# One written order for a whole half of the kernel, and late row blocks in rounded parts

## The chip, the cores and the metric

The kernel runs on one NeuronCore of a Trainium2 chip. The metric is the device time of one execution in microseconds (us); lower is better. The engines are TensorE (PE: matrix products; PEld: the loading of their weights), VectorE (DVE), ScalarE (ACT) and GpSimd (POOL). SyncE (SP) issues nearly all DMAs. Each engine works through its own queue in order, and engines wait for each other through semaphores. TensorE writes to PSUM, eight banks of 128 x 512 fp32; GpSimd doesn't touch PSUM here.

## The reference

```python
# x: 2048 x 512;  Wr, Wi: 2048 x 257;  w_gate, w_up: 512 x 1376;  w_down: 1376 x 512
h   = x + irfft2(rfft2(layernorm(x)) * (w_r + 1j * w_i))
n   = layernorm(h)
out = h + (gelu(n @ w_gate) * (n @ w_up)) @ w_down      # gelu: tanh form
```

All inputs and the output are fp32.

## The kernel before

The 2048 rows are 16 row blocks of 128 rows (row 16 p + b is partition p of block b). The work has four stages, each with an order that is written out as a list of short names; a name stands for one instruction or a few on one engine, and the list gives the order of each engine's queue.

1. START (to about 30 us): layer norm and the transform over the rows, with symmetric halves folded.
2. SECOND (to about 74 us): the transform over the columns, the product with the filter, and the way back over the rows' inner part. GpSimd and ScalarE meanwhile prepare the weights of hidden tiles 0 and 1.
3. FIRST (to about 121 us): the way back for row blocks 0 to 7 (the first half), the residual, the second layer norm, the transposition, and hidden tiles 0 and 1, each in two halves of 256 columns. `U8` to `U15` do the first step of the way back for the late blocks 8 to 15, and `K` unfolds three of them (8, 12, 9) on GpSimd: four 256-wide sums and differences, lines 830 to 833.
4. Two halves over rows. The first half (to about 279 us) multiplies row blocks 0 to 7 with hidden tiles 2 to 10 and adds up the down products; between these, the late blocks are finished. The second half does the same for row blocks 8 to 15, by an order of its own (SECOND_HALF), and ends at 438.6 us.

**A hidden tile.** The gate and up products of one tile of 128 hidden columns are seven block products (a Winograd form, for eight of the plain one), P0 to P6 (`products`, line 632). fp32 accuracy is reached by splitting each factor into a rounded high part (fp32r) and the remaining low part: `mm3` (lines 163 to 165) multiplies high x high, high x low and low x high. One block product is six matmuls of 128x128 by 128x512. A tile lies in three banks: 0 to 2 or 3 to 5, by turns. `tile_of` (line 664) has what follows each product: c1, c2, c3 copy a bank to SBUF (ScalarE, L673); d1, dy, d2 add (VectorE, L676); G0, G1 are gelu (ScalarE, L679); m0, m1 multiply (VectorE, L682); i0, i1 round the high parts (ScalarE, L688), and o0, o1 subtract for the low parts (VectorE, L695). P2 waits for c1, P4 for c2 and P5 for c3, since they add to the bank that was copied.

**A tile's weights** (`load_gu`, line 196). Two DMAs bring four raw blocks into one buffer (`raw`, a single one); GpSimd makes three more by four 256-wide sums (L207 to L215); in the first half VectorE then rounds all seven with one cast (L223), and GpSimd subtracts for the low parts in three steps, of 256, 768 and 768 columns (L228). With `by=act`, used in the second half, ScalarE rounds in three steps (L227), and each is followed by its subtract. `load_d` (line 504) loads a tile's down weights, rounds on ScalarE (L509) and subtracts on GpSimd (L511); three buffers.

**Down products** (`down`, line 754). Tiles are added up in groups (two tiles, then three, three, three). For each row block: three matmuls for each tile of the group into bank 6 or 7 (L769), then VectorE adds to `gh` (L775, or L772 with the output's DMA for the last group).

**Late blocks** (`late`, line 967). GpSimd unfolds (five of them here), SP loads the block's x, TensorE multiplies the block by the table `mis` in plain fp32 (L977: one product, which the trace shows as two records), VectorE adds the residual (L978) and takes the statistics (L520, L522). `normed` scales on ScalarE, and `combine` (line 545) transposes and makes the seven combinations `cb` for the second half.

**What sets the order there.** In the first half only TensorE's order is written (the loop at the end, lines 1243 to 1303, under `manual_schedule(engines={et.PE})`); the order on the other engines comes from a planner, with a few instructions tied to others by `issue_after` and `behind`. `rp` holds ten row buffers ("row"), given out in turn.

Of the kernel before, what the change touches and what calls it, by code (L numbers as in the profile page):

```python
# [20 lines left out]
P = 128  # L21
# [28 lines left out]
u0.1 u4.0 w4 C4.0 V4.2 X4 w0 C0.1 V0.3 X0 U1.2 C1.4 V1.0 X1 r0 U5.3 C5.5 V5.1 M4.1 O4.0 M0.2 O0.1 U2.3 H4 H0 X5 C2.5  # L50
V2.3 M5.1 H5 I4 G4 O5.0 G0 I0 S4 S0 A4 A0 E0.5 U7.2 C7.1 M1.3 O1.1 g0awh H1 Q0 N0 U6.0 C6.0 V7.4 X2 U3.4 C3.5 I5 G5 S5
M2.1 V6.3 R00 I1 G1 S1 A5 A1 R01 U9.7 C9 H2 X7 V3.1 X3 T00 a0 Q1 T01.2 s0.0 O2.1 U8.4 C8 E1.6 N1 R11 M7.0 c0 d0 f0
U12.3 e0.1 k0 R10 H7 b0 O7.0 g0 h0 C12 X6 M6.4 H6 i0 j0 T11.1 s1.2 r1 l0 T10 c1 d1 G2 I2 M3.2 O3.1 H3 G7 a1 b1 I7 S7
O6.0 U15.3 C15 e1.0 f1 g1 U14.5 C14 U10.4 C10 m0 k1 n1 g0aP0 g0ac1 g1aP0 l1 g0aP3 g0aP1 G3 I3 S3 A7 A3 Q3 g0aP2 I6 n0
G6 h1 g1ac1 E3.7 N3 g1aP2 i1 R31 T31.5 g1aP1 o1 R30 T30 S2 S6 A6 A2 g1ac2 j1 E2.6 Q2 N2 o0 g1aP4 g0awl s3.6 c3 g0ac2
g0aP4 R20 T20 a3 g1ac3 g1aP5 d3 e3.4 K9.5 m1 g0ad1 g0ac3 g0aP5 f3 b3 h3 g0ady g0aP6 i3 j3 R21 T21.7 g3 g1aP3 a2 b2
g0bP0 g0bP1 g1bP0 K12.4 g1ad1 g1ady g1aP6 r2 l3 k3 s2.8 g1aG0 c2 d2 f2 e2.7 k2 g1bP1 g1am0 g0bc1 g2 g0bP2 g1bc1 r3 n3
n2 o3 g1bP2 g0ad2 o2 g0aG0 g0am0 l2 m2 m3 g0bP3 h2 K8.4 g0aG1 g0am1 g0bc2 g0bP4 g1bd1 i2 j2 g1bc2 g1bP4 g1bG0 g1ad2
g0bc3 g0bd1 g0bdy g0ai0 g0ao0 g1aG1 g1bP3 g1ai0 g1am1 g1bc3 g1bdy g0ai1 g0ao1 g0bP6 g0bd2 g1awh g1awl g1ai1 g0bG1
g0bP5 hc g1bP6 lo1 lo2 g0bG0 g0bm0 g0bi0 g1bP5 g1bm0 g1bi0 g1bd2 g1bG1 g0bo0 U13.7 C13 lo3 g0bm1 g0bi1 U11.6 C11 g1bm1  # L60
g1bi1 g1ao0 g0bo1 g1bo0 g1bo1 g1ao1 g2P0
# [5 lines left out]
b7 b8 p15 f14 b9 h f15 b10 h b11 b12 b13 b14 b15 h  # L67
"""
# [51 lines left out]
def kernel(  # L120
# [75 lines left out]
    def load_gu(f, slowly=False, after=None, by=None, raw=None):  # L196
# [20 lines left out]
        if slowly:  # L217
            for m in range(7):
                split(r[:, 0, m], r[:, 1, m], t[:, m], pool)
                yield  # L220
        else:
            if not by:
                dve.tensor_copy(r[:, 0], t)  # L223
                yield
            for m in (slice(0, 1), slice(1, 4), slice(4, 7)):
                if by:
                    by.activation(r[:, 0, m], t[:, m], AF.Copy)  # L227
                pooled["lo"] = pool.tensor_tensor(r[:, 1, m], t[:, m], r[:, 0, m].bitcast(F32), op=ALU.subtract)  # L228
                yield
# [274 lines left out]
    def load_d(f, after=None):  # L504
        t = w3.tile([P, D], F32, name="wdr", bufs=1)
        nc.sync.dma_start(t, wd[f])
        wds[f] = r = w3.tile([P, 2, D], F32R, name="wd", bufs=3)
        with tc.issue_after(after.ins) if after else ExitStack():
            act.activation(r[:, 0], t, AF.Copy)  # L509
        yield  # L510
        pool.tensor_tensor(r[:, 1], t, r[:, 0].bitcast(F32), op=ALU.subtract)  # L511
        yield
# [203 lines left out]
    def gate_up(n):  # L716

        do = products(n)[1] if n == 2 else tile_of(n)

        def all_of(names):  # L720
            for k in names.split():
                ins = do[k]()
            return ins

        all_of("P0")
        if n == 2:

            yield
            do = tile_of(n)
            all_of("c1 P1 d1")  # L730
        else:
            all_of("c1")
            yield
            all_of("P1 d1")
        yield
        for names in ("P2 c2", "P3"):
            all_of(names)
            yield
        last = copied[n] = all_of("P4 c3")
        all_of("dy")  # L740
        yield

        for _ in load_d(tiles[n][1], last):
            pass

        for names in ("P5", "P6 d2"):
            all_of(names)
            k = names[1] == "6"
            with tc.issue_after(last.ins):
                do[f"G{k:d}"]()  # L750
            all_of(f"m{k:d} i{k:d} o{k:d}")
            yield

    def down(group, last):


        banks = {}

        def add(i, fs, c=slice(0, D)):

            b = i
            r = slice(i % 4 * P, (i % 4 + 1) * P)
            if fs[0] == group[0]:
                banks[i] = next(bank_67)
            o = ps[:, banks[i], : c.stop - c.start]
            for f in fs:
                for ha, hw in ((0, 0), (0, 1), (1, 0)):
                    start, stop = f == group[0] and ha + hw == 0, f == group[-1] and ha == 1
                    pe.matmul(o, parts_of[tiles.index((0, f))][:, ha, i // 4, r], wds[f][:, hw, c], start=start, stop=stop)  # L769
            if fs[-1] == group[-1]:  # L770
                if last:
                    dve.scalar_tensor_tensor(gh[:, b, c], o, mv[:, b, 0:1], gh[:, b, c], op0=ALU.add, op1=ALU.add)  # L772
                    nc.sync.dma_start(o3[:, b, c], gh[:, b, c])
                else:
                    dve.tensor_tensor(gh[:, b, c], o, gh[:, b, c], op=ALU.add)  # L775

        if last:

            for fs in (group[:-1], group[-1:]):
                for i in range(2):  # L780
                    add(i, fs)
                    yield
        for i in range(2 if last else 0, 7):
            add(i, group)
            yield

        add(7, group)
        yield

    tiles = [(q, f) for q, order in enumerate(orders) for f in order]  # L790
    downs = iter(())
    begun_tiles, wds, parts_of, hns, copied, sums = {}, {}, {}, {}, {}, {}
    bank_67 = itertools.cycle((6, 7))
# [150 lines left out]
    raw2 = load_gu(2)  # L944
    next(raw2)
    for k in ("r0", "r1", "r2", "r3", "hc", "lo1", "lo2", "lo3"):
        do[k] = lambda: next(raw2)

    def step(n):

        if n not in begun_tiles:
            f = tiles[n][1]
            if f not in gu:
                for _ in load_gu(f):
                    pass
            begun_tiles[n] = gate_up(n)
        next(begun_tiles[n])

    do["g2P0"] = lambda: step(2)
    et = mybir.EngineType  # L960
    with tc.manual_schedule(engines={et.PE, et.Activation, et.DVE, et.Pool}):
        for op in FIRST.split():
            name, *place = op.split(".")
            do[name](*map(int, place))


    def late(b):

        if b not in BY_THEN:

            with held("lo"):
                unfolded(b, row())
        yield
        xt = row()
        behind(nc.sync.dma_start(xt, x3[:, b]), pooled["raw"])
        py = ps[:, next(bank_67)]
        pe.matmul(py, mis[:, b], gh[:, b], start=True, stop=True)  # L977
        dve.scalar_tensor_tensor(gh[:, b], xt, mv[:, b, 0:1], py, op0=ALU.subtract, op1=ALU.add)  # L978
        for _ in stats2(b):
            pass  # L980
        yield

    def normed(b):

        hn = row()
        act.activation(hn, gh[:, b], AF.Copy, scale=rs2[:, b : b + 1])
        return hn

    def fill(n):
        for _ in range(n):  # L990
            next(downs, None)


    def second_half():
# [160 lines left out]
        yield  # L1155
# [86 lines left out]

    lates = {2: (9, 13), 3: (10,), 4: (14,), 5: (11,), 6: (15,)}
    ending = [late(b) for b in BY_THEN[:2]]
    for g in ending:
        next(g)
    downs = down(orders[0][:2], False)
    with tc.manual_schedule(engines={et.PE}):
        for n in range(2, NF):
            at_change = n == NF - 1  # L1250
            step(n)
            if n > 8:
                for i in range(2 * n - 18, 2 * n - 16):
                    with tc.issue_after(copied[n - 1].ins):
                        hns[i] = [normed(b) for b in (8 + i, 12 + i)]
            step(n)
            if at_change:
                second = second_half()
                with held("lo"):
                    next(second)  # L1260

                steps = [in_turn(i, hns[i], banks) for i, banks in enumerate(((3, 4), (5, 0), (3, 4), (1, 2)))]
                next(steps[0])
            for g in ending:
                next(g)
            if n in (6, 7):

                norm_scales(2 * n - 4, 2)
            if n == 7:
# [3 lines left out]
                for to, a in zip(kept_rows, (sd, mv[:, NB // 2 :, 0])):  # L1273
                    nc.sync.dma_start(to.rearrange("b n -> n b"), a)
# [155 lines left out]
```

## Time and profile before

| | us |
|---|---|
| median of three runs (lowest, highest) | 440.63 (440.52, 440.65) |
| the profiled execution's own time | 440.44 |
| its span, first to last instruction | 438.6 |

Busy times overlap between engines. A group's row has line, engine, operation, output<-inputs, shape and count, then busy time and mean duration in ns, then the idle time of the engine just before such instructions and what ended it. A row in order of time has start, duration, engine, line and operation; idle time before it and its releaser stand in brackets. Matmuls are pipelined: a 128x512 matmul's record is 0.39 us long, but the next one starts after 0.227, so the spacing is what TensorE pays. In the chain of waits each piece is given with the time that it adds.

### The profile page before, as it was taken

What the parts mean: (1) busy time and instruction counts of PE and PEld (TensorE: products, weight loads), DVE (VectorE), ACT (ScalarE), POOL (GpSimd) and SP (SyncE); (2) the same over time, 40 slices, a digit from 0 to 9 for tenths busy, and PEclk for the clock granted to TensorE, in tenths of its full rate; (3) what the DMA queues carried; (4) which work ended last, traced back from release to release, by engine and by line L of the source; (5) the groups of instructions that cost most, each with busy time, mean ns of one, the idle gap of its engine ahead of it and who ended that gap; (6) DMA issues with size and microseconds to landing.
All of it is one profiled execution on the core that took longest, in us unless ns stands there. A gap on an engine that the chain in (4) does not pass through costs nothing.

```text
span 438.6 us, 6625 instructions
## 1 busy us (share of the span) xinstructions
PE 432.1 (99%) x2275; PEld 366.6 (84%) x2275; DVE 313.3 (71%) x577; ACT 243.0 (55%) x502; POOL 314.5 (72%) x346
## 2 busy tenths in 40 slices
PE   8999999999999999999999999999999999999996
PEld 8998999789978777877888888888888888888885
DVE  5968976897864766368734579578677786687785
ACT  5989785799712442124432787376455653565640
POOL 6987896999859788648644944067879779787821
PEclk9999999999999999999999999999999999999999
DMA  8996904320022112112220203501212021200005
GB/s 290 386 414 105 360 27 143 129 73 24 25 96 97 49 55 89 48 50 72 72 73 24 72 25 120 169 11 62 73 48 72 26 71 49 72 24 2 0 2 192
DMA packets 23542, 41.60 MB, mean 95 GB/s; under 512 B 4178, under 2 KB 9810, under 8 KB 23380
## 3 DMA queue, kind: packets, MB, share of 16 engines
q1 hardware_dynamic: 23220, 40.92, 28.0%
q8 instruction: 18, 0.29, 0.3%
q10 hardware_dynamic: 288, 0.26, 0.2%
q14 instruction: 16, 0.13, 0.1%
HBM read 36.97 MB, written 4.20 MB: 94 GB/s over the span
## 4 chain that ended last, share of the span: by engine, by line
PE 90%; POOL 4%; DVE 1%; issue 1%; DMA 1%; ACT 0%; SPq 0%; DVEq 0%; POOLq 0%
PE ps L163 16%; PE ps L165 16%; PE ps L164 16%; PE ps L769 14%; PE ps L1108 11%; PE ps L425 4%; PE ps L437 3%; PE ps L464 3%; PE ps L530 3%; POOL pn L339 2%; POOL pn L338 2%; PE ps L869 2%; PE ps L977 1%; DMA gh<-in_x 1%; PE ps L1214 1%
## 5 line engine op out<-in xcount | busy, mean ns | idle before, releaser
L163 PE MATMUL ps<-cb,gu 128*128 128x512 f32 (+1 forms) x336 | 127.2, 379 | 0.3 <-DVE a L695 0.3
L165 PE MATMUL ps<-cb,gu 128*128 128x512 f32 (+1 forms) x336 | 124.9, 372 | 0.0
L164 PE MATMUL ps<-cb,gu 128*128 128x512 f32 (+1 forms) x336 | 124.8, 372 | 0.0
L673 ACT ACTIVATE s<-ps 128x512 f32<-128x512 f32 (+1 forms) x72 | 40.5, 562 | 87.1 <-PE ps L165 86.7
L228 POOL TENSOR_TENSOR gu<-raw,gu 128x768 fp32r<-128x768 f32 (+1 forms) x42 | 61.3, 1481 | 29.1 <-DVE gu L223 16.8
L163 PEld LDWEIGHTS ps<-cb,gu 128*128 128x128 f32 x336 | 63.3, 188 | 12.2 <-issue 1.0
L164 PEld LDWEIGHTS ps<-cb,gu 128*128 128x128 f32 x336 | 63.3, 188 | 11.8 <-issue 1.0
L165 PEld LDWEIGHTS ps<-cb,gu 128*128 128x128 f32 x336 | 63.3, 188 | 11.1
L769 PE MATMUL ps<-wd,a 128*128 128x512 f32 x264 | 63.6, 393 | 0.0
L769 PEld LDWEIGHTS ps<-wd,a 128*128 128x128 f32 x264 | 49.1, 188 | 11.6 <-DVE gh L978 1.0
L682 DVE TENSOR_TENSOR ps<-ps,s 128x512 f32<-128x512 f32 (+1 forms) x48 | 31.1, 651 | 28.1 <-PE ps L165 25.3
L1115 DVE TENSOR_TENSOR gh<-ps,gh 128x512 f32<-128x512 f32 x66 | 44.3, 682 | 0.8 <-PE ps L1108 0.8
L679 ACT ACTIVATE s<-s 128x512 f32<-128x512 f32 (+1 forms) x48 | 28.4, 594 | 20.8 <-DVE s L676 20.7
L775 DVE TENSOR_TENSOR gh<-ps,gh 128x512 f32<-128x512 f32 x24 | 16.6, 691 | 25.8 <-PE ps L769 25.8
L676 DVE TENSOR_TENSOR s<-ps,s 128x512 f32<-128x512 f32 (+1 forms) x48 | 30.7, 641 | 5.8 <-PE ps L165 4.7
L511 POOL TENSOR_TENSOR wd<-wdr,wd 128x512 fp32r<-128x512 f32 x12 | 15.6, 1298 | 17.1 <-ACT wd L509 17.1
L676 DVE TENSOR_TENSOR ps<-ps,s 128x512 f32<-128x512 f32 (+1 forms) x24 | 15.7, 654 | 16.1 <-ACT s L673 15.6
L688 ACT ACTIVATE a<-ps 128x512 fp32r<-128x512 f32 (+1 forms) x26 | 13.8, 533 | 17.1 <-DVE ps L682 17.1
L207 POOL TENSOR_TENSOR raw<-raw 128x256 f32<-128x256 f32 x16 | 11.9, 741 | 15.6 <-DMA raw<-in_wgu 13.9
L1021 POOL TENSOR_TENSOR t<-mis,t 128x768 fp32r<-128x768 f32 (+1 forms) x9 | 13.3, 1479 | 13.3 <-ACT t L1019 13.2
L429 ACT ACTIVATE dp<-ps 64x512 f32<-64x512 f32 x32 | 19.0, 593 | 4.0 <-PE ps L425 3.6
L453 POOL TENSOR_TENSOR z<-t,t 128x520 f32<-128x520 f32 x15 | 19.5, 1298 | 2.1 <-DVE t L445 2.1
(183 smaller groups left out, 896.7 us busy)
## 6 DMA issues: line engine op xcount, KB each, us to landing
wt<-in_w SPq DMA_DIRECT2D x16, 520.0 KB, 7.2
raw<-in_wgu SPq DMA_DIRECT2D x32, 256.0 KB, 3.0
out<-gh SPq DMA_DIRECT2D x15, 256.0 KB, 2.0
gh<-in_x SPq DMA_DIRECT2D x7, 512.0 KB, 8.8
row<-in_x SPq DMA_DIRECT2D x12, 256.0 KB, 2.8
wdr<-in_wd SPq DMA_DIRECT2D x12, 256.0 KB, 2.6
mis<-in_wd SPq DMA_DIRECT2D x10, 256.0 KB, 2.7
a<-in_wgu SPq DMA_DIRECT2D x8, 256.0 KB, 3.1
```

Source lines behind the costliest of these rows:

```text
L163: pe.matmul(o, lh, rh, start=(i == 0 and not onto), stop=False, skip_group_check=True)
L164: pe.matmul(o, lh, rl, start=False, stop=False, skip_group_check=True)
L165: last = pe.matmul(o, ll, rh, start=False, stop=(i == n - 1), skip_group_check=True)
L228: pooled["lo"] = pool.tensor_tensor(r[:, 1, m], t[:, m], r[:, 0, m].bitcast(F32), op=ALU.subtract)
L453: eng.tensor_tensor(z[:, :, first], t1[:, :, first], t2[:, :, first], op=ALU.add)
L673: return lambda: act.activation(to, a, AF.Copy)
L676: return lambda: dve.tensor_tensor(to, a, b, op=ALU.add)
L679: return lambda: act.activation(g, g, AF.Gelu_apprx_tanh)
L682: return lambda: dve.tensor_tensor(u, u, g, op=ALU.mult)
L769: pe.matmul(o, parts_of[tiles.index((0, f))][:, ha, i // 4, r], wds[f][:, hw, c], start=start, stop=stop)
L1108: pe.matmul(ps[:, k], w[:, hw], a[ha], start=start and hw + ha == 0, stop=hw == 1, skip_group_check=True)
L1115: by.tensor_tensor(to, o, to, op=ALU.add)
```

## The change

- FIRST is written in another order, without the cast of tile 2's weights (`hc`), which ScalarE now rounds too; its last entry, `g2P1`, stands for tile 2's c1, P1 and d1.
- A new list, FIRST_HALF, gives the order of TensorE, ScalarE, VectorE and GpSimd for the rest of the first half, in place of the written TensorE loop and the planner. FIRST and FIRST_HALF are issued under one `manual_schedule`.
- Names of the new list: `tNPk`, `tNc1` and so on are tile N's steps as above; `yN.0` to `yN.10` load and prepare tile N's weights (DMA; four sums on GpSimd; then ScalarE and GpSimd by turns, three times); `wN.0` to `wN.2` the down weights; `Kb` unfolds block b; `ub` rounds it (ScalarE) and `vb` makes its low part (GpSimd); `mh` and `ml` do the same once for the table (128 x 1024); `Lb` loads x, `Yb@k` is the block's product into bank k, now of three matmuls; `Rb` and `Bb` are residual and statistics; `Dgi@k` and `Egi` are the down product and the sum for row block i and group g (`F` the last tile's part); `H` and `i` are the scaling and the combinations, `N` the norm's scales, `S0` the rows kept for the second half, `Z` the second half's first loads.
- The rounded parts of a late block take two row buffers each. Rounded table parts lie in a tile `t`.
- The second half's own order is as before.

The diff, cut to its core (of the long lists, the stretches that matter below):

```diff
 FIRST = """
...
+g1bP2 g1aG0 e2.7 k2 n2 g1ad2 o3 g0bc2 h2 o2 m2 l3 i2 g0am0 g0bG0 g1bd1 g0bP3 g1bc2 g0bP4 g0ai1 g1aG1 j2
+g0bc3 g0bdy g1bP4 g1bP3 g0ai0 g1bc3 g1awh g0bP5 m3 g1am0 g0bP6 K8.4 lo1 g1ai0 g1bdy g1bG0 g1bP6 g0ao0 g1ao0 g0ao1
+g0bd2 lo2 lo3 U13.7 g0bG1 g1bP5 U11.6 g0bm0 g0bi0 g1bd2 g1bG1 g0bm1 g0bi1 g0bo0 g2P0 C13 g1am1 g1ai1 g1bm0 g1bi0 g0bo1
+g1awl C11 g1bm1 g1bi1 g1bo1 g1ao1 g1bo0 g2P1
 """
...
+FIRST_HALF = """
+u8 t2P3 t2P2 v8 mh ml Y8@6 u12 v12 y3.0 y3.1 y3.2 t2c2 L8 L12 u9 Y12@7 t2P4 R12 D01@7 y3.3 y3.4 R8 D00@6 y3.5 y3.6
+t2c3 t2dy t3P0 y3.7 y3.8 w2.0 t3P1 t2P5 y3.9 y3.10 E00 w2.1 w2.2 D02@6 t3c1 t3P2 v9 K13 y4.0 y4.1 B8.0 t3c2 B12.0 y4.2
+y4.3 E02 t2G0 t3P3 E01 D03@7 E03 t2P6 t3P4 t3d1 u13 v13 L9 L13 t2d2 t2m0 D04@6 B8.1 E04 y4.4 y4.5 y4.6 y4.7 y4.8 y4.9
+t2i0 y4.10 t3c3 D05@7 t3dy D06@6 E05 t4P3 K10 w3.0 D07@7 w3.1 w3.2 y5.0 t2o0 t4P0 t2G1 t2m1 t2i1 E06 t4c1 t3P5 t4P2
+u10 v10 E07 Y13@7 t3G0 t3m0 Y9@6 t2o1 t4P1 R13 y5.1 t4c2 B12.1 t4P4 t4d1 t4G0 R9 t3i0 t3P6 t3d2 L10 w4.0 K14 t4c3 t4P5
+y5.2 y5.3 u14 v14 y5.4 y5.5 Y10@6 Y14@7 w4.1 t4dy t4P6 y5.6 y5.7 t3o0 t5P0 t4m0 t4i0 t4o0 y5.8 t5P3 L14 R14 y5.9 y5.10
...
+L11 K15 t6P0 y7.0 y7.1 w5.0 y7.2 y7.3 y7.4 E13 t5P6 B14.1 t6c1 t4i1 t4o1 D15@7 t5d2 t5G1 t5m1 u15 t6P2 t6P1 E15 D14@6
...
+H11 H20 H21 t8G0 t8m0 w8.0 t9P0 t9c1 t7o1 D25@7 y10.0 D24@6 E24 y10.1 t8P6 y10.2 y10.3 y10.4 y10.5 y10.6 y10.7 t9P2
...
+"""
...
             for m in (slice(0, 1), slice(1, 4), slice(4, 7)):
                 if by:
                     by.activation(r[:, 0, m], t[:, m], AF.Copy)
+                    if apart:
+                        yield
                 pooled["lo"] = pool.tensor_tensor(r[:, 1, m], t[:, m], r[:, 0, m].bitcast(F32), op=ALU.subtract)
                 yield
...
-    raw2 = load_gu(2)
+    raw2 = load_gu(2, by=act)
...
-    def late(b):
-
-        if b not in BY_THEN:
-
-            with held("lo"):
-                unfolded(b, row())
-        yield
-        xt = row()
-        behind(nc.sync.dma_start(xt, x3[:, b]), pooled["raw"])
-        py = ps[:, next(bank_67)]
-        pe.matmul(py, mis[:, b], gh[:, b], start=True, stop=True)
-        dve.scalar_tensor_tensor(gh[:, b], xt, mv[:, b, 0:1], py, op0=ALU.subtract, op1=ALU.add)
...
-    with tc.manual_schedule(engines={et.PE}):
-        for n in range(2, NF):
...
+        def back_s(k):
+            nonlocal py
+            py = ps[:, k]
+            for hm, hu in ((0, 0), (1, 0), (0, 1)):
+                pe.matmul(py, mi2[:, hm, b - NB // 2], parts[hu], start=hm + hu == 0, stop=hu == 1)
...
+        def part(h):
+            parts[h] = rp.tile([P, D], F32R, name="row")
+            if h:
+                pool.tensor_tensor(parts[1], gh[:, b], parts[0].bitcast(F32), op=ALU.subtract)
+            else:
+                act.activation(parts[0], gh[:, b], AF.Copy)
...
+        mi2 = w3.tile([P, 2, NB // 2, P], F32R, name="t", bufs=1)
+        act.activation(mi2[:, 0], mis[:, NB // 2 :], AF.Copy)
+
+    later["mh"] = high_of_mi
+    later["ml"] = lambda: pool.tensor_tensor(mi2[:, 1], mis[:, NB // 2 :], mi2[:, 0].bitcast(F32), op=ALU.subtract)
...
+    with tc.manual_schedule(engines={et.PE, et.Activation, et.DVE, et.Pool}):
+        for op in FIRST.split():
+            name, *place = op.split(".")
+            do[name](*map(int, place))
+        for op in FIRST_HALF.split():
+            name, _, place = op.partition("@")
+            later[name](*([int(place)] if place else []))
     with tc.manual_schedule(engines={et.PE, et.Activation, et.DVE, et.Pool}):
         next(second, None)
```

## Prediction before the run

> **What bounds the kernel now.** I read the page's busy times first, then the busy time by stretch, then the groups by shape, the chain of waits, and last the instructions in order of time where TensorE waits.
>
> ```profile
> span 438.6 us, 6625 instructions
> ...
> PE 432.1 (99%) x2275; PEld 366.6 (84%) x2275; DVE 313.3 (71%) x577; ACT 243.0 (55%) x502; POOL 314.5 (72%) x346
> ```
>
> By stretch (the stretch, then PE, PEld, DVE, ACT and POOL busy with their instructions, then TensorE's clock and the DMAs):
>
> ```profile
> 116.00:168.00 52.00, 51.68 (x231) 40.81 (x230) 35.17 (x59) 16.85 (x33) 40.28 (x42) 1.00 0.25 81
> 168.00:220.00 52.00, 52.00 (x225) 41.96 (x224) 32.41 (x69) 14.74 (x26) 34.75 (x37) 1.00 0.18 56
> ```
>
> The reader is to see that TensorE is never idle in the stretches that the change rewrites, at full clock. So two things alone can move the time: work that TensorE no longer does, and waits that TensorE gets. In 116 to 168 us GpSimd has 12 us free of 52, ScalarE 35.
>
> **The work that goes.** Each late block's fp32 product becomes three products of rounded parts.
>
> ```profile
> 123.84 0.87 PE ps L977 x2
> ...
> 134.17 2.72 PE ps L769 x12
> ```
> ```profile
> L977 PE MATMUL ps<-gh,mis 128*128 128x512 f32 x16 | 7.8, 591 | 0.0
> ```
>
> The chain of waits gives 0.87 us for one fp32 product (two records) and 2.72 / 12 = 0.227 us for one product of rounded parts. Eight blocks: 8 x (0.87 - 3 x 0.227) = **1.5 us less**. Below I write 1.36 for a tile product (six of 0.227), 2.04 for a down product of nine, 0.68 for a late block.
>
> The Trainium skill (FP8 and Floating Point Precision, section TensorE Precision Notes) says that true fp32 makes four passes through the array, among them low times low. By that the change saves one pass of 0.227 a block, 1.8 us in all, and the sum would be 0.3 us lower; the row of 0.87 differs a little from four passes (0.91), and I go by the row.
>
> **The wait that goes.** At 119 us TensorE stands before tile 2's first product.
>
> ```profile
> 118.33 0.83 PE L530 MATMUL ps<-dis,gh 128*128 128x128 f32 x6
> 119.44 0.50 PE L163 MATMUL ps<-cb,gu 128*128 128x512 f32 x1 [0.27 <-DVE a L695]
> ```
> ```profile
> 115.92 2.14 DVE L223 CAST gu<-raw 128x1792 fp32r<-128x1792 f32 x1
> ...
> 118.97 0.41 DVE L695 TENSOR_TENSOR a<-ps,a 128x256 fp32r<-128x256 f32 x1
> ```
> ```profile
> 115.80 1.31 POOL L511 TENSOR_TENSOR wd<-wdr,wd 128x512 fp32r<-128x512 f32 x1
> ```
> ```profile
> L223 DVE CAST gu<-raw 128x1792 fp32r<-128x1792 f32 x9 | 10.9, 1207 | 2.4 <-PE ps L164 1.3 <-POOL raw L215 1.1
> ```
>
> The cast took 2.14 us beside a GpSimd subtract, against (10.9 - 2.14) / 8 = 1.10 for the other eight; VectorE came late to the low part that ended at 119.38, and TensorE started 0.06 later. The product's first matmul shows 0.50 where its followers show 0.39, so idle and slow start are 0.27 + 0.1 or a little more: **0.4 us less**, since ScalarE now rounds. What is late next there is the copy behind the product, which is in the next part.
>
> **Work that is only moved to idle engines.**
>
> ```profile
> L227 ACT ACTIVATE gu<-raw 128x768 fp32r<-128x768 f32 x10 | 8.4, 844 | 0.0
> ...
> L227 ACT ACTIVATE gu<-raw 128x256 fp32r<-128x256 f32 x5 | 2.0, 403 | 0.0
> ```
> ```profile
> raw<-in_wgu SPq DMA_DIRECT2D x32, 256.0 KB, 3.0
> ```
>
> Rounding a tile's weights costs ScalarE 0.40 + 2 x 0.84 = 2.1 us, some 19 for nine tiles, where VectorE paid 10.9; the eight 512-wide rounded parts 8 x 0.63 (the row of a 512-wide rounding below); the high part of the table (128x1024) between 0.84, its 768-wide row, and twice that. ScalarE's 35 free us cover these, except where one stands in front of something urgent (below). The loads are the same ones; the next raw tile lands in 3.0 us and its first user stands 5.4 us of GpSimd work behind it.
>
> **The work that comes.** GpSimd gets eight low parts of blocks (1.25 each) and the low part of the table. Of these, six and the table fall where 116 to 168 us is now: 40.3 + 6 x 1.25 + 2.4 = 50.2 of 52 us. So GpSimd has no reserve left just where it makes the tiles' low parts. I walked the new list there, and priced each step by these rows:
>
> ```profile
> 133.78 0.39 PE L165 MATMUL ps<-cb,gu 128*128 128x512 f32 x1
> ```
> ```profile
> 119.41 0.58 ACT L823 ACTIVATE gh<-ps 128x512 f32<-128x512 f32 x1
> 119.89 0.38 ACT L688 ACTIVATE a<-ps 128x256 fp32r<-128x256 f32 x1
> ...
> 134.21 0.60 ACT L673 ACTIVATE s<-ps 128x512 f32<-128x512 f32 x1 [9.73 <-PE ps L165]
> ...
> 188.44 0.63 ACT L509 ACTIVATE wd<-wdr 128x512 fp32r<-128x512 f32 x1 [2.39 <-PE ps L769]
> ```
> ```profile
> 127.57 0.68 DVE L775 TENSOR_TENSOR gh<-ps,gh 128x512 f32<-128x512 f32 x1
> 128.16 0.17 DVE L522 BATCH_NORM_AGGREGATE mv<-bn 128x2 f32<-128x6 f32 x1
> ...
> 134.84 0.70 DVE L676 TENSOR_TENSOR ps<-ps,s 128x512 f32<-128x512 f32 x1 [1.32 <-ACT s L673]
> ```
> ```profile
> 126.16 0.74 POOL L207 TENSOR_TENSOR raw<-raw 128x256 f32<-128x256 f32 x1 [3.69 <-DMA raw<-in_wgu]
> 126.98 0.74 POOL L211 TENSOR_TENSOR raw<-raw 128x256 f32<-128x256 f32 x1
> ...
> 189.15 1.30 POOL L511 TENSOR_TENSOR wd<-wdr,wd 128x512 fp32r<-128x512 f32 x1 [6.05 <-ACT wd L509]
> ...
> 301.37 1.30 POOL L1044 TENSOR_TENSOR a<-row,a 128x512 fp32r<-128x512 f32 x1 [1.40 <-ACT a L1039]
> 302.62 0.74 POOL L228 TENSOR_TENSOR gu<-a,gu 128x256 fp32r<-128x256 f32 x1
> ```
> ```profile
> L228 POOL TENSOR_TENSOR gu<-raw,gu 128x768 fp32r<-128x768 f32 x28 | 51.4, 1852 | 8.4 <-ACT gu L227 6.4 <-issue 1.9
> ```
>
> A last matmul at 133.78 lets its reader start at 134.21, 0.20 after its step of 0.227. ScalarE hands to VectorE 0.03 after its record's end, to GpSimd 0.08. Behind each other, ScalarE's 512-wide steps are 0.48 apart, VectorE's 0.60, GpSimd's 1.25; GpSimd's dependent 256-wide ones 0.82, its 768-wide ones 1.81 (0.04 less than their record, as with the 512-wide). The 1024-wide subtract has no row: 1.30 and 1.85 (512 and 768) extended give 2.4, two 512-wide ones 2.5.
>
> *Wait 1, block 8's products.* Zero is the end of t2P0. ScalarE copies (c1) at 0.20; u8 stands behind it: 0.68 to 1.31; v8 starts on GpSimd at 1.39, ml at 2.64 and ends at 5.04; TensorE could go on at 5.10. It reaches ml's product after t2P1, t2P3, t2P2 and one product: 4.31. It waits 0.8, and for v12 (ends 6.29, with TensorE there at 6.01) another 0.3: **1.1 us**.
>
> *Wait 2, tile 3.* GpSimd goes on at 6.24 with y3.1 to y3.4 (to 9.44), hands to ScalarE's y3.5 and gets it back: y3.6 is 9.95 to 10.69. ScalarE's y3.7 stands behind t2c3 and ends at 11.10; y3.8 runs 11.18 to 13.03. TensorE (P4, D01, D00 and t3P0 after Y12) is at t3P0 at 10.66 and at t3P1 at 12.1: waits of 0.1 and 1.0, **1.1 us**.
>
> *Wait 3, t4P2.* w3.1 rounds into a buffer that D07 frees, and holds ScalarE's queue: from D07's end w3.1 at 0.20, t2G1 at 0.72 to 1.35, VectorE's t2m1 to 2.07, t2i1 at 2.10, t4c1 at 2.58 to 3.18. TensorE has t4P0 and t3P5, 2.72: **0.5 us**.
>
> *Wait 4, t5P3.* From y3.8's end to y5.8's end GpSimd's queue holds four 768-wide steps (7.2), three blocks' unfolding (four 256-wide steps each, 8.7), six 512-wide steps (7.5) and ten 256-wide ones (7.5): 31 us, and some 3.3 us in which it waits for ScalarE or a row buffer (1.3 of it for u10, behind wait 3), so 34.2. TensorE needs 22 x 1.36 + 4 x 0.68 + 0.5 = 33.2: **0.8 us** (the difference less handover).
>
> *Wait 5, D15.* t6c1 waits for t6P0 and holds t4i1: 0.20 + 0.48 + 0.60 + 0.03, then t4o1 0.68 and handover 0.06 = 2.05, against one product, 1.36: **0.7 us**. *Wait 6, D25.* E22, t8m0 and t7o1 queue on VectorE: 0.20 + 0.60 + 0.60 + 0.68 + 0.06 = 2.14 against t9P0's 1.36: **0.8 us**.
>
> For none of these is there other TensorE work in the list to fill in, and lost TensorE time isn't regained later, as it stays at 99%. The second half keeps its order, and its first products find their inputs 0.4 us or more early by the same walk.
>
> The sum is -1.5 - 0.4 + 1.1 + 1.1 + 0.5 + 0.8 + 0.7 + 0.8 = +3.1. The profiled execution took 440.44 us around its span of 438.6, so it would become 443.5; the median of the runs shown is 440.63, 0.2 more, and would become **443.7 us**, my forecast.
>
> **The rivals.** *The waits don't arise* (faster): what decides is how early each feeder starts. If the engines run ahead of TensorE, no wait remains and the gain stands: 440.6 - 1.9 = 438.7. For it speaks that ScalarE is free two thirds of the time; against it that waits 1, 3, 5 and 6 each begin at a TensorE product and can't start earlier. It is faster by 0.2% (0.9 us) only if waits under 1.0 us remain in all.
> *GpSimd is quicker than its rows* (same): waits 2, 4 and the 0.3 of v12 go, the others stay: 443.7 - 2.2 = 441.5, and down to 440.7 with 0.8 off the rest. It takes a GpSimd some 10% shorter over 50 us, and the free 12 us of before speak for some room.
> *Row buffers* (slower still): the first half asks for 41 row buffers instead of 25, of ten; each TensorE wait frees them later, GpSimd and the loads stand behind, and tiles 6 to 8 get waits such as tile 5's, 2 x 0.8 to 1.0, so 1.8 in all: 445.5. For it speaks that the walk already shows GpSimd waiting for a row before K14; against it that its queue is some 5 us ahead at tile 6.
>
> The Trainium skill (SBUF — State Buffer, section Who interferes with whom) says that VectorE and GpSimd share one exclusively locked port pair, and that VectorE instructions with at most one SBUF input, outside two-port modes, stay clear of it. The slow cast above agrees; by that rule GpSimd's twelve added us (8 x 1.25 + 2.4) cost VectorE nothing once the casts are gone, so I add no price for it.
>
> **How the numbers follow.** The walk as it stands 0.70, row buffers 0.10, quicker GpSimd 0.10, no waits 0.10. The range reaches from the quicker GpSimd, 440.6, to the row buffers, 445.6; the walk's own is 442.0 to 445.0, with wait sums between 3.5 and 6.5. About 0.2% can be told from no change. Slower 0.80, same 0.10, faster 0.10.
>
> **What would show it.** Late blocks: 24 products of 0.227 instead of 16 fp32 records. No cast on VectorE, and none of the wait at 119. TensorE idle before the products of mi2 and rows, released by GpSimd, about 1.1; before L163 by GpSimd about 1.9; before the down products by VectorE 1.5; GpSimd over 95% busy for 50 us after tile 2 begins. TensorE without idle time in the first half makes the prediction wrong, and so does a second half that is longer than before.

## The result: 1.05 us slower, and a second half that got longer

| | before | after |
|---|---|---|
| median, nine runs each (us) | 440.63 | 441.68 |
| lowest, highest | 440.47, 440.98 | 441.58, 442.15 |
| ratio after to before | | 1.0024, interval 1.0014 to 1.0034 |

The forecast was 443.7: the sign is right, the size is a third of what was forecast, and as the following shows, the sum was wrong in more places than that says. In each later group of runs the kernel before took 440.55 to 440.65 us again. The head of the page of the changed kernel, and its busy time by stretch (columns as for the kernel before):

```profile
span 439.9 us, 6676 instructions
...
PE 432.8 (98%) x2283; PEld 368.1 (84%) x2283; DVE 303.5 (69%) x568; ACT 263.3 (60%) x538; POOL 327.1 (74%) x355
```
```profile
116.00:168.00 52.00, 51.26 (x238) 41.90 (x237) 26.47 (x50) 26.67 (x50) 48.89 (x47) 1.00 0.23 77
168.00:220.00 52.00, 52.00 (x229) 42.66 (x228) 29.18 (x61) 23.46 (x41) 38.68 (x41) 1.00 0.21 71
```

The work moved as forecast: VectorE 35.2 to 26.5 us in the first stretch, ScalarE 16.9 to 26.7, GpSimd 40.3 to 48.9 of 52 (50.2 was forecast). TensorE is idle for 0.74 us in all between 116 and 220 us. So most of the forecast waits (5.0 us in all) can't be there, and yet the time went up.

**Where the time went.** TensorE's last piece, and the first late product of the second half, in order of time, before and then after:

```profile
295.56 0.61 PE L1108 MATMUL ps<-row,t 128*128 128x512 f32 x2
...
433.72 0.76 PE L1214 MATMUL ps<-a,wd 128*128 128x256 f32 x5
```
```profile
295.66 0.62 PE L1029 MATMUL ps<-row,t 128*128 128x512 f32 x2
...
434.82 0.75 PE L1135 MATMUL ps<-a,wd 128*128 128x256 f32 x5
```

At the second half's first late product the changed kernel is 0.1 us behind; at the end, 1.1. The second half loses 1.0 us, though its order and its waits are those of before. The chain of waits shows it at the same products of the second half, before and after:

```profile
329.73 0.68 PE ps L1108 x3
331.76 0.68 PE ps L1108 x3
```
```profile
329.85 0.70 PE ps L1029 x3
331.93 0.70 PE ps L1029 x3
```

Three products take 0.70 us instead of 0.68, at a granted clock of 1.00 from 280 to 434 us in both kernels. At full resolution of the records the steps of 512-wide products are 226 or 227 ns nearly everywhere before; after, long stretches have steps of 224 to 237 ns, 230.5 to 231 in the mean. What these steps take over 226.7 ns adds up to 0.6 us from 116 us on before and 2.6 us after, 1.0 of it in the second half. After three or more steps of 226 or 227 ns, a longer one comes at 32 places, and in 29 of them the product reads `wd`.

What the change does to `wd`: a tile that the prediction passed over. The kernel before allocates `sd`, 32 bytes of each partition, after everything else; the changed kernel allocates it early, with 64 bytes, and the tiles behind it move up. The start addresses in a partition, as the program's allocation lists them:

```
tile   before            after
sd     227648 (behind)   213056
wd     215360            215424     (first of three, 4096 bytes apart)
gu      48192             48192     = 64 above a multiple of 256
cb     104512            104512     = 64 above a multiple of 256
row, t, a                            64 above a multiple of 256 in both
```

Before, every operand of the rounded products lies 64 bytes above a multiple of 256. After, `wd` alone lies 128 above. (`wdr`, the raw down weights, moves with it, but TensorE doesn't read it.)

### The profile page after: what moved, and what is told of

Read it like the earlier page. It is cut to its first block, busy times and chain, and to the rows that moved or that the text cites. A ratio compares the mean times of both kernels' runs of the same rounds, so it can differ in the third digit from the quotient of the medians.

```text
span 439.9 us, 6676 instructions
## 1 busy us (share of the span) xinstructions
PE 432.8 (98%) x2283; PEld 368.1 (84%) x2283; DVE 303.5 (69%) x568; ACT 263.3 (60%) x538; POOL 327.1 (74%) x355
## 4 chain that ended last, share of the span: by engine, by line
PE 91%; ACT 4%; DMA 2%; issue 1%; POOL 1%; SPq 0%; DVE 0%; DVEq 0%; ACTq 0%
PE ps L190 16%; PE ps L188 16%; PE ps L189 16%; PE ps L1227 14%; PE ps L1029 11%; PE ps L452 4%; PE ps L558 3%; PE ps L464 3%; PE ps L491 3%; DMA gh<-in_x 2%; PE ps L821 2%; PE ps L1135 1%; ACT ts L407 1%; PE ps L1198 1%; ACT ms L357 1%
## 5 line engine op out<-in xcount | busy, mean ns | idle before, releaser
L701 ACT ACTIVATE s<-ps 128x512 f32<-128x512 f32 (+1 forms) x72 | 40.3, 561 | 58.3 <-PE ps L190 58.0
L252 ACT ACTIVATE gu<-raw 128x768 fp32r<-128x768 f32 (+1 forms) x42 | 28.3, 697 | 10.9 <-DMA raw<-in_wgu 5.7
```

The source lines that it names most:

```text
L701: return lambda: act.activation(to, a, AF.Copy)
```

## The experiments

**e1, sd of 128 bytes.**

```diff
-    sd = w3.tile([P, NB], F32, name="sd", bufs=1)[:, : NB // 2]
+    sd = w3.tile([P, 2 * NB], F32, name="sd", bufs=1)[:, : NB // 2]
```

> The changed kernel with one number altered: the small tile sd takes 128 bytes of each partition instead of 64, so that the three wd tiles behind it begin 64 bytes above a multiple of 128, as in the kernel before and as every other operand of TensorE's rounded products; in the changed kernel they begin on a multiple of 128. Theory A (addresses): in the trace of the changed kernel the 512-wide steps of 228 to 236 ns begin, in 29 of 32 places, at a product that reads wd, and add up to 2.2 us over 227 ns a step, against 0.2 before. They go, and the time falls by 2.0 us to 439.7, below the kernel before (440.63). Rival B (traffic: GpSimd's and ScalarE's added work slows TensorE's reads): the work is the same, so the time stays at 441.7. Rival C (TensorE's clock is a little lower in this program): 441.7 too. By either theory the wait before the products of mi2 (1.1 us) stays.

Measured: 442.31 us, slower still (1.0037, 1.0025 to 1.0050). The period of 128 bytes was wrong; but the time did move with nothing altered than 64 bytes of an allocation, and the sum of the long steps rose from 2.6 to 3.4 us. Rivals B and C had no change to offer.

**e2, the kernel before with sd where the change has it.**

```diff
     do["g2P0"] = lambda: step(2)
+    sd = w3.tile([P, NB], F32, name="sd", bufs=1)[:, : NB // 2]
...
-                sd = w3.tile([P, NB // 2], F32, name="sd", bufs=1)
```

> The kernel before with one piece of the change alone: sd is allocated where the change allocates it and with its 64 bytes, ahead of wd, so that wd begins on a multiple of 128. Order and work are those of before. Theory A (addresses): 264 + 99 rounded products read wd, and steps of 228 to 236 ns appear at them: 440.63 + 2.0 = 442.6, in the second half about 1.1 of it. Rivals B and C: nothing that they speak of changes, 440.6.

Measured: 442.61 us (1.0045, 1.0032 to 1.0057), 2.0 more than before, as forecast. The same stretch of the chain, here of e2, has the long triples without any of the change's work:

```profile
326.70 0.68 PE ps L1109 x3
328.74 0.70 PE ps L1109 x3
330.81 0.70 PE ps L1109 x3
```

**e3, the down products of block 0 moved ahead of block 8's.**

```diff
-u8 t2P3 t2P2 v8 mh ml Y8@6 u12 v12 ... u9 Y12@7 t2P4 R12 D01@7 y3.3 y3.4 R8 D00@6 y3.5 y3.6
+u8 t2P3 t2P2 D00@6 v8 mh ml u12 v12 ... u9 Y8@7 t2P4 E00 Y12@6 R8 D01@7 y3.3 y3.4 R12 y3.5 y3.6
```

> The changed kernel with five names of its list moved: TensorE does the first block's down products (D00) before block 8's three products, and tile 2's fifth product between the products of blocks 8 and 12, so that GpSimd's low parts (ml, v8, v12) have 2.7 us more. Work and addresses are unchanged. Theory (the wait of 1.1 us before the products of mi2 is TensorE time lost, and nothing is behind it): 441.7 - 1.1 = 440.6. Rival (GpSimd is the bound over these 50 us, and the wait comes back at tile 3's first products, 131 to 134 us): 441.7, with the same 1.1 us before L188.

Measured: 441.31 us, 0.4 less than the changed kernel: between the two. The runs of both overlap a little (441.18 to 441.89, and 441.58 to 442.15), so the reading rests on the rows. The wait before block 8 is gone, and this has come before tile 3's products, in order of time:

```profile
130.71 0.39 PE L189 MATMUL ps<-cb,gu 128*128 128x512 f32 x1
131.12 0.50 PE L190 MATMUL ps<-cb,gu 128*128 128x512 f32 x1
...
132.38 0.39 PE L189 MATMUL ps<-cb,gu 128*128 128x512 f32 x1
132.92 0.50 PE L190 MATMUL ps<-cb,gu 128*128 128x512 f32 x1 [0.16 <-POOL gu L255]
```

Steps of 0.41 and 0.54 instead of 0.23, and a slow one behind each: 0.7 us. So GpSimd's work is the bound there. The forecast's waits 1 and 2 are one lack of GpSimd time; where wait 1 stands, it gives GpSimd what wait 2 would have asked for.

**e4, e1 and e3 together.**

> Both edits, the 128 bytes for sd and the moved down products. If addresses and the wait are two separate terms: 441.7 - 2.0 - 1.1 = 438.6, two us below the kernel before. If the address effect only fills time in which TensorE would wait for GpSimd anyway, less than the sum: 439.6 or more.

Measured: 441.95 us, 0.4 below e1, as e3 is 0.4 below the changed kernel. The two terms are separate; both sizes in the expectation fell with e1 and e3.

**e5, sd behind wd again; e6, sd of 256 bytes; e7, sd behind and all operands moved by 64 bytes.**

```diff
-    sd = w3.tile([P, NB], F32, name="sd", bufs=1)[:, : NB // 2]
...
     def keep_rows():
+        sd = w3.tile([P, NB // 2], F32, name="sd", bufs=1)
```
```diff
-    sd = w3.tile([P, NB], F32, name="sd", bufs=1)[:, : NB // 2]
+    sd = w3.tile([P, 4 * NB], F32, name="sd", bufs=1)[:, : NB // 2]
```
```diff
-    eps = base.tile([P, 32], F32, name="eps")[:, :1]
+    eps = base.tile([P, 48], F32, name="eps")[:, :1]
```

> The 128 bytes were no cure (442.31, steps longer still), so the theory that only the phase against 128 bytes counts has fallen: wd moved by 64 bytes costs 2.0 us, by 128 bytes 2.7. Here the changed kernel has sd allocated where the kernel before allocates it, behind wd, with its 32 bytes: wd stands at the very addresses of before, and nothing else is altered. Theory A2 (the address of wd, by a longer period): 441.7 - 2.0 = 439.7, and steps over 227 ns add up to 0.3 us at most. Rival B (traffic of GpSimd and ScalarE): 441.7, since the work and its order are the changed kernel's; the moved kernel before, at 442.6 without that work, already speaks against it.

> The changed kernel with sd of 256 bytes: wd stands 256 bytes above its place in the kernel before, so that all operands of the rounded products lie 64 bytes above a multiple of 256, as before. If the period is 256 bytes or a divisor, 439.7. If the very place or a longer period counts (512 bytes, say), the time is 441.7 or more.

> sd behind wd as in e5, and a tile at the bottom of the memory (eps) 64 bytes larger: all operands of the rounded products move by the same 64 bytes, and keep their distances. If what counts is that the operands differ in phase, the time is that of e5, 439.7. If the phase itself counts (64 above a multiple of 256 is good, 128 is not), all 1320 products of 512 columns slow down, 3.5 times the number that reads wd: 439.7 + 3.5 x 2.0 = 446.7.

Measured: 439.24, 439.22 and 439.22 us, each faster than the kernel before (0.9970, 0.9969 and 0.9970; intervals 0.9958 or 0.9960 to 0.9981). The change without the 64 bytes gains 1.4 us, and the 64 bytes cost 2.4. The longest run of down products, 57 in one piece, in the chain of waits; one row each of the changed kernel, e5, e6, e7 and e1:

```profile
263.67 13.06 PE ps L1227 x57
```
```profile
262.33 12.94 PE ps L1226 x57
```
```profile
262.22 12.94 PE ps L1227 x57
```
```profile
262.38 12.95 PE ps L1226 x57
```
```profile
263.78 13.29 PE ps L1227 x57
```

57 x 0.2267 is 12.92; the changed kernel pays 0.2291 a product, e1 0.2332. In e7 `wd` lies 128 above a multiple of 256, as in the changed kernel, and nothing is lost, since the other operands lie there too: it is the operands' distances that count. By the Trainium skill (TensorE: Matmul & The Clock Gate, Step-by-step: what each phase is for) TensorE has two independent read ports, and loading the next weights takes no read bandwidth from the running matmul. Nothing there depends on addresses, and by it e1, e2 and e5 to e7 would have changed nothing; the measurements decide otherwise.

**e12, sd of 32 bytes at the changed kernel's place.**

```diff
-    sd = w3.tile([P, NB], F32, name="sd", bufs=1)[:, : NB // 2]
+    sd = w3.tile([P, NB // 2], F32, name="sd", bufs=1)
```

> The changed kernel with sd of 32 bytes at the changed kernel's place: wd moves by 32 bytes against the kernel before. Measured so far: by 0 bytes 439.24 us, by 64 bytes 441.68, by 128 bytes 442.31, by 256 bytes 439.22, all operands together by 64 bytes 439.22. If the cost grows with the distance: 440.5. If any distance that isn't a multiple of 256 costs about the same: 441.7. If lines of 64 bytes count, and 32 bytes stay in one: 439.2, though a row of 512 bytes then takes nine lines instead of eight.

Measured: 442.62 us (1.0043, 1.0029 to 1.0056), 3.4 above e5: the shortest distance costs the most. The same 57 products take

```profile
263.96 13.31 PE ps L1227 x57
```

So neither a cost that grows with the distance nor lines of 64 bytes fits. By 0, 32, 64, 128 and 256 bytes: 0, 3.4, 2.4, 3.1 and 0 us.

**e8, low parts of the table and of blocks 8 and 12 by VectorE** (on e5; t2d1 put behind them).

```diff
+    BY_DVE = (8, 12)
-                pool.tensor_tensor(parts[1], gh[:, b], parts[0].bitcast(F32), op=ALU.subtract)
+                (dve if b in BY_DVE else pool).tensor_tensor(parts[1], gh[:, b], parts[0].bitcast(F32), op=ALU.subtract)
...
-    later["ml"] = lambda: pool.tensor_tensor(
+    later["ml"] = lambda: dve.tensor_tensor(
...
-u8 t2P3 t2P2 v8 mh ml Y8@6 u12 v12 y3.0
+mh ml u8 v8 u12 v12 t2d1 t2P3 t2P2 Y8@6 y3.0
```

> e5 with VectorE in GpSimd's place for the low parts of the table (ml) and of blocks 8 and 12, in an order in which the table comes first; GpSimd has 5 us less to do between 122 and 127 us. Moving the down products forward in e3 took away the 1.3 us of waits before blocks 8 and 12, but 0.7 us came back before tile 3's first products, released by GpSimd. Theory (GpSimd's time is what TensorE lacks there): both waits go, at most 0.2 us is left, and 439.7 - 1.2 = 438.5. Rival (VectorE's two-input work stands in GpSimd's way, as the cast of 2.14 us in the kernel before did): the three instructions take about twice their time, ml 2.5 us and more instead of 1.2, and TensorE waits for VectorE instead: 439.5 or more.

Measured: 438.86 us (0.9962, 0.9949 to 0.9975), 0.4 below e5, with runs that overlap a little. Both waits for GpSimd are gone; a new one, 0.87 us with the slow step behind it, stands before the next down products, and VectorE's row says what it is:

```profile
127.93 0.50 PE L1228 MATMUL ps<-wd,a 128*128 128x512 f32 x1 [0.60 <-DVE gh L1202]
```
```profile
122.19 1.22 DVE L1282 TENSOR_TENSOR t<-mis,t 128x1024 fp32r<-128x1024 f32 x1 [1.03 <-ACT t L1279]
123.33 1.84 DVE L1212 TENSOR_TENSOR row<-gh,row 128x512 fp32r<-128x512 f32 x2
...
127.13 1.41 DVE L1202 SCALAR_TENSOR_TENSOR gh<-row,mv,ps 128x512 f32<-128x512 f32 x2 [1.36 <-DMA row<-in_x]
```
```profile
123.68 0.94 POOL L232 TENSOR_TENSOR raw<-raw 128x256 f32<-128x256 f32 x1 [2.40 <-DMA raw<-in_wgu]
124.69 1.07 POOL L236 TENSOR_TENSOR raw<-raw 128x256 f32<-128x256 f32 x1
125.85 0.74 POOL L238 TENSOR_TENSOR raw<-raw 128x256 f32<-128x256 f32 x1
```

The residual of block 12 waits for its x row, which landed at 127.1. VectorE and GpSimd do hinder each other here, where both have two SBUF inputs: a subtract of 512 columns took VectorE 0.92 us beside GpSimd's sums, against 0.61 for 512 columns of ml (1.22 for 1024), which ran while GpSimd waited; GpSimd's sums took 0.94 and 1.07 beside them instead of 0.74. That agrees with the Trainium skill (SBUF — State Buffer, Who interferes with whom), by which a VectorE instruction with two SBUF inputs contends with a GpSimd one that reads SBUF. But ml, alone, took 1.22 us, not the 2.5 of the rival.

**e9, late products in fp32 again** (on e5; u, v, mh and ml left out of the list).

```diff
-            for hm, hu in ((0, 0), (1, 0), (0, 1)):
-                pe.matmul(py, mi2[:, hm, b - NB // 2], parts[hu], start=hm + hu == 0, stop=hu == 1)
+            pe.matmul(py, mis[:, b], gh[:, b], start=True, stop=True)
```

> On e5 (439.24, sd behind wd), the late blocks' products are undone: one fp32 product each from the unrounded table and rows, as in the kernel before, and the rounded parts, high and low (u, v, mh, ml), are left out. Theory, the prediction's first term: an fp32 product with what it does to the first rounded product behind it costs 0.87, three rounded ones 0.68, so 8 x 0.19 = 1.5 more, and up to 0.3 for the longer steps that follow each fp32 product in the trace of before; less the 1.3 us of waits for GpSimd's parts before blocks 8 and 12: 439.24 + 0.2 to 0.5 = 439.4 to 439.7. Rival (the three products gain nothing beside the fp32 one): only the wait goes, 438.0.

Measured: 439.99 us, 0.75 above e5. With e5's wait of 1.3 us gone, undoing the products costs 2.0 us, more than the 1.5 of the forecast. At full resolution 1.6 of it stands at the fp32 products and in the steps right behind them, and 0.2 in three late steps between 353 and 358 us that e5 doesn't have. After the fp32 products the first rounded one has a step of 0.63, and longer steps follow:

```profile
153.63 1.88 PE L1196 MATMUL ps<-gh,mis 128*128 128x512 f32 x4
154.94 0.79 PE L188 MATMUL ps<-cb,gu 128*128 128x512 f32 x1
155.57 0.40 PE L189 MATMUL ps<-cb,gu 128*128 128x512 f32 x1
```

**e10, three down steps with their products in reverse** (on e5).

```diff
+            turn = -1 if (g, i) in ((0, 7), (1, 5), (2, 5)) else 1
+            order = [(f, ha, hw) for f in group for ha, hw in ((0, 0), (0, 1), (1, 0))][::turn]
```

> On e5 (439.24), three of the down steps (D07, D15, D25) take their products in the reverse order, last tile's low part first; work and lists are the same. Theory (the prediction's waits 3, 5 and 6 don't arise because a step needs its late operand, or frees its buffer, only part of the way through): now D07 frees the first tile's wd only with its sixth product, and D15 and D25 need their latest input with their first one; waits of 0.4 before t4P2 (about 153 us), 0.7 before D15 (183 us) and 0.7 before D25 (228 us) appear: 439.24 + 1.8 = 441.0. Rival (the engines are simply quicker or further ahead than the walk put them): no waits, 439.2.

Measured: 441.08 us, 1.8 above e5. Two waits are there, of 0.8 and 0.9 us with the slow step behind each:

```profile
183.72 1.45 PE L1228 MATMUL ps<-wd,a 128*128 128x512 f32 x5 [0.54 <-DVE a L723]
...
229.68 0.50 PE L1228 MATMUL ps<-wd,a 128*128 128x512 f32 x1 [0.61 <-DVE a L723]
```

The third isn't: with the order reversed, tile 3's down weights were given the other buffer, which then comes free at the same moment. Wait 3's reason was so not tested here. That the time came out at the 441.0 of the expectation is luck: two waits longer than expected stand for three.

**e11, e8 with the down products moved ahead.**

```diff
-mh ml u8 v8 u12 v12 t2d1 t2P3 t2P2 Y8@6 y3.0 ... u9 Y12@7 t2P4 R12 D01@7 y3.3 y3.4 R8 D00@6 y3.5 y3.6
+mh ml u8 v8 u12 v12 t2d1 t2P3 t2P2 D00@6 y3.0 ... u9 Y8@7 t2P4 E00 Y12@6 R8 D01@7 y3.3 y3.4 R12 y3.5 y3.6
```

> e8 (438.86) with the down products moved ahead as in e3. In e8 the waits for GpSimd are gone, and 0.87 us stands before the next down products instead: VectorE waits until 127.1 us for the x row of block 12, issued at 122 behind the tile's weights and landing 4.8 us later. With D00 ahead, its bank is needed 1.4 us later. Theory: the 0.87 goes down to 0.2 at most: 438.1. Rival (the bound there is the sum of the transfers, and the wait moves on to tile 3's first products, whose weights were issued before the rows): 438.8.

Measured: 437.85 us, 0.9936 of the kernel before (0.9924 to 0.9949): 2.8 us faster than before, 3.8 faster than the changed kernel. The 0.87 is gone, and nothing came back at tile 3. TensorE is without idle time from 116 to 220 us (busy 52.00 in both stretches):

```profile
116.00:168.00 52.00, 52.00 (x244) 43.40 (x243) 29.62 (x52) 26.92 (x51) 46.14 (x47) 1.00 0.27 87
168.00:220.00 52.00, 52.00 (x231) 43.07 (x230) 30.81 (x69) 25.13 (x44) 39.14 (x39) 1.00 0.18 61
```

## Why the prediction was wrong

The prediction's first step was that "two things alone can move the time", work that goes and waits that come. A third did, the spacing of products whose work and waits are unchanged. And of the six waits only the first came. Without the third thing the change is a gain (e5), so the sign of the forecast came out right by luck, not by its mechanism.

- **Late products (-1.5).** Right in kind. 24 products of rounded parts are there, one group of them in the rows (`L1198`); but the term was too small, 2.0 instead of 1.5. At full resolution the kernel before pays 7.5 us for its fp32 products with the late steps behind them, against 24 x 0.2267 = 5.4. The forecast took 0.87 for each and left out the long steps that follow (0.25 in all) and a late start of 0.3 behind the first two blocks.
- **The wait at 119 (-0.4).** Gone. Tile 2's first product starts at 119.10 instead of 119.44, and between 118.8 and 119.1 in the traces of all experiments with the new list but e3 (119.35).

```profile
119.10 0.47 PE L188 MATMUL ps<-cb,gu 128*128 128x512 f32 x1
```

- **Work moved to idle engines (0).** Right for ScalarE: no wait of TensorE is put down to its rounding.
- **Wait 1 (+1.1).** Right: it is there, in the forecast's place and by its releaser. The second product of block 8 starts 1.05 after the first, 0.83 late; three more late steps make it 1.3.

```profile
124.67 0.39 PE L1198 MATMUL ps<-row,t 128*128 128x512 f32 x1
125.72 1.76 PE L1198 MATMUL ps<-row,t 128*128 128x512 f32 x5 [0.67 <-POOL t L1280]
```

- **Wait 2 (+1.1).** Not there. The step that failed: GpSimd "hands to ScalarE's y3.5 and gets it back". The first block of the raw weights isn't altered by the four sums, so ScalarE rounded it before they began, and GpSimd went from the sums to the low part without a pause. The copy t2c3 and y3.7, behind y3.5 in ScalarE's queue, came earlier too, and GpSimd didn't wait for y3.7 either:

```profile
125.94 0.41 ACT L252 ACTIVATE gu<-raw 128x256 fp32r<-128x256 f32 x1
...
129.40 1.57 ACT L252 ACTIVATE gu<-raw 128x768 fp32r<-128x768 f32 x2
```
```profile
126.88 0.74 POOL L232 TENSOR_TENSOR raw<-raw 128x256 f32<-128x256 f32 x1
...
129.34 0.75 POOL L240 TENSOR_TENSOR raw<-raw 128x256 f32<-128x256 f32 x1
130.04 2.56 POOL L255 TENSOR_TENSOR gu<-raw,gu 128x256 fp32r<-128x256 f32 x2
```

The first 768 columns are ready at 132.6, TensorE needs them from 132.9. It was near: without wait 1, 0.7 us of wait 2 comes back (e3).
- **Wait 3 (+0.5).** Not there. The step "D07's end w3.1 at 0.20": D07 reads the first tile's weights in its first three products, and w3.1 starts 0.22 after these (149.44 + 3 x 0.23 = 150.12).

```profile
149.44 1.55 PE L1227 MATMUL ps<-wd,a 128*128 128x512 f32 x6
```
```profile
150.34 0.63 ACT L537 ACTIVATE wd<-wdr 128x512 fp32r<-128x512 f32 x1 [4.34 <-PE ps L1227]
```

- **Wait 4 (+0.8).** Not there. The 31 us of GpSimd's work were right; the term "some 3.3 us in which it waits" was too large. GpSimd's idle times between 138 and 163 us are 1.26 (before v10) and 0.46: ScalarE again rounds the first block of tiles 4 and 5 before their last sum, as with wait 2. The 768 columns end at 165.3, TensorE reaches them at 165.9.
- **Waits 5 and 6 (+0.7, +0.8).** Not there. The walk held a whole down step until its last input was there. D15 and D25 need tile 4's and tile 7's low part with the last of nine products only; D25 starts before VectorE does the part:

```profile
229.11 0.68 DVE L723 TENSOR_TENSOR a<-ps,a 128x512 fp32r<-128x512 f32 x1
```
```profile
229.10 4.29 PE L1227 MATMUL ps<-wd,a 128*128 128x512 f32 x18
```

e10 puts the product first that reads it, and gets both waits, 0.82 and 0.89: the durations of the walk were good, its grain was not.
- **What was left out (+2.4).** The list of edits has the rows kept for the second half (`S0`) but not where their tile now lies. The statement "the second half keeps its order" was taken for "keeps its time". The prediction names as a sign against itself a second half longer than before, and that is what came.
- **The range.** The walk's own range counts from the profiled execution's 440.44 us and the forecast from the median, so the range is 0.2 us low; nothing hangs on it.

The sum as measured: -2.0 (the fp32 products), -0.3 to -0.5 (the start of tile 2), +1.3 (wait 1), +2.4 (e5), together +1.2 to +1.4 against 1.05; 0.2 to 0.4 us is not accounted for. Without the addresses the change is a gain of 1.4 us, 0.5 short of what the rival without waits gave (438.7 against e5's 439.24), which had no wait 1 either. Forecast and result are nearer to each other than their terms, because 3.9 us of waits that didn't come and 2.4 us of a cost that wasn't seen partly cancel.

## What to carry to other kernels

Walk a list by instructions, not by its names: a step may begin before its last input and free its first buffer before its end, and the five waits that failed were made from whole steps, or from a whole buffer of which one block was free. An allocation is part of a change: compare the start addresses of TensorE's operands before and after, and where unchanged code got longer without a new wait, look at the spacing of its instructions. A wait that goes is a gain only as far as the engine behind it has time to spare; here GpSimd had not, and work had to move off it.

## What the runs showed of the hardware

The pace of TensorE's rounded 128x512 products depends on where their operands lie in the partition relative to each other. With all of them a multiple of 256 bytes apart a product takes 226.7 ns; with the 363 products' `wd` 32, 64 or 128 bytes off, 228 to 241 in long stretches (0.2335, 0.2291 and 0.2332 us in the 57 products), also in products behind these that don't read `wd`. The granted clock was 1.00 in both. In the down products `wd` is the moving operand and in the second half's the weights, and both start long stretches. That the weight load of the next product and the stream of the running one meet in some way is an idea that would fit; it wasn't tried, and neither was a distance between 128 and 256 bytes. Steps of 228 to 236 ns, for some ten products, also follow the fp32 products of the kernel before and of e9.
